# Moving the output weights ahead of group 3, loading two groups ahead of the DMA transposes, and 64-token blocks from group 3 on, in a fused linear-attention and SwiGLU kernel

## The chip, the cores and the metric

One core of a Trainium2 chip runs the whole program. The metric is the device time of one execution in microseconds (us). Most executions of a kernel agree within a per cent or so; some fall into a slower state. Each run is therefore marked fast or slow, and ratios use fast runs alone. A quoted median is of all runs; where some were slow, the text says so.

## The reference, cut to what matters

Batch 4, 8 heads, 768 tokens, head size 64. A linear attention with a decay per head works through the tokens in blocks of 64. Its output, 3072 tokens of 512 columns, goes through a SwiGLU feed-forward (FFN) of width 1536.

```python
for b in range(nb):                       # blocks of 64 tokens
    intra = einsum('bhic,bhjc->bhij', qb, kb) * Dmask
    intra = einsum('bhij,bhjd->bhid', intra, vb)
    inter = einsum('bhid,bhde->bhie', qb * lam_pow, kv_state)
    out[:, :, sl] = intra + inter
    kv_state = lam_block * kv_state + einsum('bhsd,bhse->bhde', kb * rev_pow, vb)
...
g = x @ w_gate; val = x @ w_val
return (g * sigmoid(g) * val) @ w_out
```

## The kernel before

A *group* is 256 tokens of one batch; there are 12. The FFN works on tiles of two groups (512 tokens), six tiles in all. TensorE runs the FFN of one tile while the attention of later groups is put in between as short insertions. To prepare a group, k, q and v are loaded, k and q are cast (q also scaled), a DMA transpose turns them (the first three groups are turned on TensorE), and GpSimd scales v. Then TensorE computes scores and the state update ("ahead"), and later the part from the state ("inter") and the part inside the block ("intra"), together the "core".

Groups below `NAT0` use blocks of 128 tokens, made of two neighbouring tokens in each partition. Their loads are one DMA each with 512-byte pieces. Groups from `NAT0` on use blocks of 64 tokens. Their loads are ten DMAs a group (four for k, four for q, two for v) with 256-byte pieces:

```python
NAT0 = 6
def load_fp32(g, eng, src, what, h0=0, h1=H):
    ...
    if g < NAT0:                      # 128-token form: one DMA
        eng.dma_start(out=t[:, h0:h1], in_=gsrc(src, g, h0)[:, 0:h1 - h0])
        return
    ...
    parts = [(0, 128, False)] if what == "v" else [(0, M, False), (M, M, True)]
    for s in range(2):                # 64-token form: 2 or 4 DMAs
        for p0, n, rev in parts:
            eng.dma_start(out=t[p0:p0 + n, :, s * D:s * D + D], in_=...)

def dma_transpose(g):                 # in the sync queue, with all loads
    nc.sync.dma_start(out=tt..., in_=t..., transpose=True)

def cast_scaled(g, eng=nc.vector):
    nc.scalar.copy(out=..., in_=st[("kraw", g)]...)          # k, on ACT
    eng.tensor_tensor(out=..., in0=st[("qraw", g)]..., ...)  # q, on VectorE
    dma_transpose(g)

def ffn_out(t, b, last=False):        # output projection and store
    ... 12 matmuls of 512 columns ...
    fn(out=osb[:, c0:c1], in_=ps)     # ACT
    eng.dma_start(out=..., in_=osb)   # ACT's queue, 256 KB

# the plan: at(step, what to do after it)
at(s0[5], load_group, 3)
at(s0[7], load_group, 4, "kq")
at(s0["11b"], cast_scaled, 3, nc.gpsimd)
at(s1a[3], cast_scaled, 4)
at(s1a[3], load_group, 5)
for c in range(0, FC, 2):
    at(s1a[3], wo_piece, c, c + 2)    # output weights behind load 5
...
at(s1b[6], ahead, 4)
at(s1b[8], wo_cast, ACTC)             # the cast that ACT waits for
at(s1b[10], core_b, 4)
```

## Time and profile before

| | before |
|---|---|
| median | 229.23 us (228.62 to 229.84) |
| span of the profiled run | 227.1 us |
| TensorE busy | 96% |
| mean granted TensorE clock | 1.000 |
| idle of TensorE at attention pieces, in all | 1.7 us on ACT's guard copy, 1.2 of it once |

The prediction below shows most lines of this profile as it reads them. On the page, the clock that the throttle granted to TensorE, one digit for each of 40 slices, is full all the way:

```profile
PEclk9999999999999999999999999999999999999999
```

### The profile page before, as it was taken

To read this page: it belongs to the slowest core of one execution; us is meant where nothing else is said; L and a number is where in the kernel's file an instruction comes from. 1 tells how busy PE (TensorE), PEld (TensorE's weight loads), DVE (VectorE), ACT (ScalarE), POOL (GpSimd) and SP (SyncE) were. 2 spreads that over 40 slices of the span, in tenths; PEclk is the share of its full clock that TensorE was granted. 3 is DMA by queue.
4 is the path that set the end of the run, shared out by engine and by line. 5 is a ranking of instruction groups with operands and counts; after the bars stand their busy time and mean duration, and the time that the engine had idled before them with its cause. 6 is when DMAs were issued, how large, how long until landed. Compare 5 with 4: busy or idle time off the path is not lost.

```text
span 227.1 us, 5890 instructions
## 1 busy us (share of the span) xinstructions
PE 218.5 (96%) x2432; PEld 118.2 (52%) x2444; DVE 90.1 (40%) x154; ACT 106.5 (47%) x209; POOL 88.2 (39%) x129
## 2 busy tenths in 40 slices
PE   7889999999979999999999999999999999999994
PEld 3556455878854444454544544544544444444443
DVE  2754357685825214545352362253242123222200
ACT  5868585754652446363454463453433423322221
POOL 6476736642793312978373092092150000000000
PEclk9999999999999999999999999999999999999999
DMA  6999999899997779799877748815101101101122
GB/s 199 345 360 377 367 354 313 210 255 352 300 219 189 206 168 222 177 200 191 217 178 186 185 98 214 214 36 139 49 3 48 46 3 46 46 0 46 49 92 92
DMA packets 88012, 39.70 MB, mean 175 GB/s; under 512 B 57650, under 2 KB 83506, under 8 KB 87986
## 3 DMA queue, kind: packets, MB, share of 16 engines
q1 hardware_dynamic: 83474, 32.64, 55.2%
q10 hardware_dynamic: 4512, 6.69, 8.3%
q8 instruction: 19, 0.31, 0.5%
q14 instruction: 7, 0.06, 0.1%
HBM read 28.31 MB, written 6.29 MB: 152 GB/s over the span
## 4 chain that ended last, share of the span: by engine, by line
PE 84%; DMA 6%; SPq 5%; issue 1%; DVE 1%; ACT 1%; DVEq 0%; ACTq 0%
PE bank L539 27%; PE bank L517 25%; PE bank L524 24%; DMA woraw<-in_moe_w_out_dram 4%; DMA qraw<-in_q_dram 2%; PE bank L475 2%; SPq L99 2%; SPq L228 2%; PE bank L462 2%; PE bank L383 1%; PE bank L353 1%; PE bank L327 1%; PE bank L290 1%; DVE ssb L334 1%; PE bank L168 0%
## 5 line engine op out<-in xcount | busy, mean ns | idle before, releaser
L527 DVE TENSOR_TENSOR h<-sil,bank 128x512 bf16<-128x512 bf16 (+1 forms) x87 | 51.4, 595 | 110.7 <-PE bank L524 94.5
L517 PE MATMUL bank<-xt,wg_sb 128*128 128x512 bf16 (+1 forms) x348 | 76.7, 343 | 0.0
L524 PE MATMUL bank<-xt,wv_sb 128*128 128x512 bf16 (+1 forms) x348 | 76.5, 342 | 0.0
L521 ACT ACTIVATE sil<-bank 128x512 bf16<-128x512 f32 (+1 forms) x87 | 45.8, 528 | 43.4 <-PE bank L517 40.4
L539 PE MATMUL bank<-wo_sb,h 128*128 128x512 bf16 (+1 forms) x288 | 64.2, 370 | 0.7 <-issue 0.2
L524 PEld LDWEIGHTS <-wv_sb 128*128 128x128 bf16 x348 | 34.0, 98 | 28.3
L517 PEld LDWEIGHTS <-wg_sb 128*128 128x128 bf16 x348 | 32.2, 98 | 27.4 <-DVE xt L487 0.5
L539 PEld LDWEIGHTS <-h 128*128 128x128 bf16 x300 | 29.1, 98 | 32.4
L541 ACT COPY osb<-bank 128x512 f32<-128x512 f32 (+1 forms) x24 | 13.8, 576 | 54.9 <-PE bank L539 52.9
L239 POOL TENSOR_TENSOR v_s<-v,dec 128x1024 bf16<-128x1024 f32 (+1 forms) x14 | 23.2, 1665 | 13.9 <-DMA v<-in_v_dram 9.5
L422 POOL TENSOR_TENSOR kvf<-kvs,ups 128x256 f32<-128x256 f32 x8 | 5.8, 726 | 45.1 <-ACT ups L405 40.1
L334 DVE TENSOR_TENSOR ssb<-bank,causal 128x512 bf16<-128x512 f32 x24 | 15.5, 684 | 3.9 <-PE bank L327 3.8
L487 ACT CAST xt<-bank 128x512 bf16<-128x512 f32 x21 | 12.8, 665 | 3.1 <-PE bank L475 2.3
L422 POOL TENSOR_TENSOR kvf<-kvf,ups 128x256 f32<-128x256 f32 x16 | 13.4, 839 | 0.6
L431 POOL CAST kvn<-kvf 64x256 bf16<-64x256 f32 x24 | 11.6, 483 | 1.5
L405 ACT COPY ups<-bank 128x256 f32<-128x256 f32 (+1 forms) x24 | 9.5, 450 | 2.3 <-PE bank L383 1.4
L259 ACT CAST qk<-kraw 128x1024 bf16<-128x1024 f32 x9 | 9.4, 1043 | 0.0
L261 DVE TENSOR_TENSOR qk<-qraw,qdn 128x1024 bf16<-128x1024 f32 x6 | 7.7, 1286 | 3.7 <-DMA qraw<-in_q_dram 3.7
L475 PE MATMUL bank<-ssb,v_s 64*64 64x128 bf16 (+1 forms) x384 | 7.2, 208 | 2.0 <-ACT guard L446 1.7
L222 POOL CAST wv_sb<-wraw 128x1024 bf16<-128x1024 f32 (+1 forms) x7 | 6.4, 918 | 6.1 <-DMA wraw<-in_moe_w_val_dram 6.0
L358 DVE TENSOR_TENSOR ssb<-bank,causaln 128x512 bf16<-128x512 f32 x12 | 8.3, 688 | 1.2 <-PE bank L353 1.1
L233 POOL CAST wo_sb<-woraw 128x1024 bf16<-128x1024 f32 x5 | 5.7, 1171 | 5.3 <-DMA woraw<-in_moe_w_out_dram 5.3
(62 smaller groups left out, 115.6 us busy)
## 6 DMA issues: line engine op xcount, KB each, us to landing
out_dram<-osb ACTq DMA_DIRECT2D x23, 256.0 KB, 2.5
v<-in_v_dram SPq DMA_DIRECT2D x16, 256.0 KB, 4.2
woraw<-in_moe_w_out_dram SPq DMA_DIRECT2D x6, 512.0 KB, 7.1
kraw<-in_k_dram SPq DMA_DIRECT2D x24, 128.0 KB, 3.2
qraw<-in_q_dram SPq DMA_DIRECT2D x24, 128.0 KB, 3.8
wraw<-in_moe_w_gate_dram SPq DMA_DIRECT2D x5, 512.0 KB, 6.6
wraw<-in_moe_w_val_dram SPq DMA_DIRECT2D x5, 512.0 KB, 7.3
kraw<-in_k_dram SPq DMA_DIRECT2D x4, 512.0 KB, 6.5
```

Of the source, the lines that this page charges most:

```text
L239: eng.tensor_tensor(out=st[("vs", g)][:, h0:h1], in0=st[("v", g)][:, h0:h1].rearrange("p h (s d) -> p h s d", s=2), in1=vfac(g, h0, h1), o ...
L334: nc.vector.tensor_tensor(out=ssb[:, h2, 2 * c:2 * c + 2].rearrange("p a s n -> p a (s n)"), in0=sp[(c, h2)].rearrange("p (a x) -> p a x", ...
L422: nc.gpsimd.tensor_tensor(out=o, in0=f, in1=u, op=ALU.add)
L431: nc.gpsimd.tensor_copy(out=o[64 - h2 * 64:128 - h2 * 64], in_=f[h2 * 64:h2 * 64 + 64])
L475: nc.tensor.matmul(op[r][h2 * 64:h2 * 64 + 64, cols(g, hp, s)], v_s[ps, 2 * hp + h2, s], ssb[ps, h2, hp * 2 + s] if g >= NAT0 else ssb[ps, ...
L487: fns[r](out=xt[:, g % 2, :, r].rearrange("p h (m s) -> p h s m", s=2) if g < NAT0 else xt[:, g % 2, :, :, r * M:r * M + M], in_=op[r].rea ...
L517: nc.tensor.matmul(gp[:, 0:N], wg_sb[:, mc, fs], xt[:, b0 // 2:b1 // 2, mc].rearrange("p g b n -> p g (b n)"), start=(mc == 0), stop=(mc = ...
L521: nc.scalar.activation(sil[:, 0:N], gp[:, 0:N], AF.Silu)
L524: nc.tensor.matmul(vp[:, 0:N], wv_sb[:, mc, fs], xt[:, b0 // 2:b1 // 2, mc].rearrange("p g b n -> p g (b n)"), start=(mc == 0), stop=(mc = ...
L527: nc.vector.tensor_tensor(out=h_sb[:, fc, b0:b1].rearrange("p b n -> p (b n)"), in0=sil[:, 0:N], in1=vp[:, 0:N], op=ALU.mult)
L539: nc.tensor.matmul(ps, h_sb[:, fc, b], wo_sb[:, fc, c0:c1], start=(fc == 0), stop=(fc == FC - 1))
L541: fn(out=osb[:, c0:c1], in_=ps)
```

## The change

The intent is to take away ACT's wait for the output weights (they come before the loads of group 3), to keep loads two whole groups ahead, and to use the cheaper 64-token insertions for groups 3 to 5 as well. The diff, cut to its core (lines that only release delayed copies, and the value scaling of group 4, are left out as well):

```diff
-    NAT0 = 6
+    NAT0 = 3
@@ cast_scaled
         dma_transpose(g)
+        load_group(g + 2)
@@ plan
-    at(s0[5], load_group, 3)
+    for c in range(0, FC, 2):
+        at(s0[5], wo_piece, c, c + 2)
-    at(s0[7], load_group, 4, "kq")
+    at(s0[7], load_group, 3)
+    at(s0[7], load_group, 4)
...
-    at(s0["11b"], cast_scaled, 3, nc.gpsimd)
-    at(s1a[3], cast_scaled, 4)
-    at(s1a[3], load_group, 5)
-    ... (scores, core and state of groups 3 to 5 in pieces)
+    at(s1a[8], cast_scaled, 3)
+    at(s1a[8], v_scale, 3, nc.gpsimd)
+    at(s1a[8], ffn_out, 0, 0)
+    at(s1a[8], ffn_out, 0, 1)
+    at(s1a[8], ffn_out, 0, 2)
+    at(s1a[8], ahead, 3)
+    at(s1a[8], cast_scaled, 4)
+    at(s1a[8], ffn_out, 0, 3)
+    at(s1a[10], core, 3, SPLIT)
+    at(s1b[5], ahead, 4)
+    at(s1b[2], cast_scaled, 5)
+    at(s1b[6], v_scale, 5, nc.gpsimd)
+    at(s1b[11], cast_scaled, 6)
+    at(s1b[11], ffn_out, 1, 0)
+    at(s1b[11], attend, 4)
+    at(s1b[11], v_scale, 6, nc.gpsimd)
+    at(s1b[11], ffn_out, 1, 1)
+    ... (the other projections, attend 5; the casts of wo spread over step 1a)
```

In the queue that gives: output weights, load 3, load 4, transpose 3, load 5, transpose 4, load 6 and so on. Group 3 is the first of its batch and has no state yet, so the change also skips the state matmuls that would multiply by zero.

More of the change, by code (lines that the diff above doesn't have):

```diff
@@ L244, in load_group @@
     def load_group(g, parts="kqv"):
+        if g >= NG:
+            return
         for src, what in ((k, "kraw"), (q, "qraw"), (v, "v")):
@@ L394, in upd_copy @@
         hd = "p (h d) -> p h d"
-        if i == 0 and 0 in parts:
+        if i == 0 and g >= NAT0:
+            st[("kv", g)] = [None]
+        elif i == 0 and 0 in parts:
             kv = kv_pool.tile([128, HP, D], BF16, name="kvn", tag="kvn1", bufs=2)
@@ L455, in inter @@
         started = set()
-        for hp, s, r, h2 in phase(g, first, (1,) if i == 0 else (0, 1) if first else (1, 0)):
+        for hp, s, r, h2 in phase(g, first, (1,) if i == 0 and g < NAT0 else (0, 1) if first else (1, 0)):
             if g < NAT0 and s:
@@ L459, in inter @@
             n = 2 * s + r if g >= NAT0 else r
+            if kv[n] is None:
+                continue
             row, hq = (1 - h2, HP - 1 - hp) if g >= NAT0 and r else (h2, hp)
@@ L477, in intra @@
                              ssb[ps, h2, hp * 2 + s] if g >= NAT0 else ssb[ps, h2, hp, s],
-                             start=((first or (i == 0 and r == 0)) and (r, h2) not in started),
+                             start=((first or (i == 0 and r == 0 and g < NAT0)) and (r, h2) not in started),
                              stop=(not first), skip_group_check=True)
@@ L556, in attend @@
             upd_copy(g + 1)
-            scores(g + 1)
+            if g + 1 >= NAT0:
+                scores(g + 1)
             late, later[:] = later[:], []
         core_b(g)
-        if g + 1 < NG:
+        if g + 1 < NAT0:
+            scores(g + 1)
+            state(g + 1)
+        elif g + 1 < NG:
             later[:] = late
@@ L684, in _body @@
     at(s0["11a"], core, 2, SPLIT)
-    at(s0["11b"], cast_scaled, 3, nc.gpsimd)
-    at(s0["11b"], v_scale, 3, nc.gpsimd)
     at(s0["11b"], state, 2)
-    at(s0["11b"], load_group, 4, "v")
+    at(s0["11b"], wo_cast)
     s1a = [step(1, fc, 0, 2) for fc in range(FC)]
     s1b = [step(1, fc, 2, 4) for fc in range(FC)]
-    at(s1a[3], cast_scaled, 4)
-    at(s1a[3], load_group, 5)
-    for c in range(0, FC, 2):
-        at(s1a[3], wo_piece, c, c + 2)
-    at(s1a[7], scores, 3, (0,))
-    at(s1a[7], run_later, 2)
@@ L698, in _body @@
-    at(s1a[8], scores, 3, (1,))
-    at(s1a[8], upd_mm, 3)
-    at(s1a[8], run_later, 2)
-    at(s1a[8], upd_copy, 3)
-    at(s1a[9], core_a, 3)
-    at(s1a[10], core_b, 3, SPLIT)
-    at(s1a[10], v_scale, 4, nc.gpsimd)
-    at(s1a[10], state, 3)
-    at(s1b[3], cast_scaled, 5)
-    at(s1b[3], load_group, 6)
-    at(s1b[4], wo_cast)
-    at(s1b[4], wo_cast)
-    at(s1b[6], ahead, 4)
-    at(s1b[6], run_later, 2)
-    at(s1b[6], wo_cast)
-    at(s1b[6], wo_cast)
-    at(s1b[6], v_scale, 5, nc.gpsimd)
@@ L715, in _body @@
-    at(s1b[8], wo_cast, ACTC)
-    at(s1b[8], wo_cast)
-    at(s1b[9], core_a, 4)
-    at(s1b[10], core_b, 4)
-    at(s1b[11], ffn_out, 0, 0)
-    at(s1b[11], ahead, 5)
-    at(s1b[11], run_later, 3)
-    at(s1b[11], ffn_out, 0, 1)
-    at(s1b[11], core_a, 5)
-    at(s1b[11], ffn_out, 0, 2)
-    at(s1b[11], core_b, 5)
+    at(s1a[1], wo_cast)
+    at(s1a[3], wo_cast, ACTC)
+    at(s1a[4], wo_cast)
+    at(s1a[5], wo_cast, ACTC)
+    at(s1a[6], wo_cast)
+    at(s1a[8], cast_scaled, 3)
+    at(s1a[8], v_scale, 3, nc.gpsimd)
@@ L726, in _body @@
+    at(s1a[8], ffn_out, 0, 0)
+    at(s1a[8], ffn_out, 0, 1)
+    at(s1a[8], ffn_out, 0, 2)
+    at(s1a[8], ahead, 3)
+    at(s1a[8], run_later, 2)
+    at(s1a[8], cast_scaled, 4)
+    at(s1a[8], ffn_out, 0, 3)
+    at(s1a[10], core, 3, SPLIT)
+    at(s1a[11], v_scale, 4, nc.gpsimd)
+    at(s1b[5], ahead, 4)
+    at(s1b[2], cast_scaled, 5)
+    at(s1b[6], v_scale, 5, nc.gpsimd)
     at(s1b[11], cast_scaled, 6)
-    at(s1b[11], load_group, 7)
+    at(s1b[11], ffn_out, 1, 0)
+    at(s1b[11], attend, 4)
@@ L728, in _body @@
+    at(s1b[11], run_later, 2)
     at(s1b[11], v_scale, 6, nc.gpsimd)
-    at(s1b[11], ffn_out, 0, 3)
-    outs = [(1, b) for b in range(4)]
+    at(s1b[11], ffn_out, 1, 1)
+    at(s1b[11], ffn_out, 1, 2)
+    at(s1b[11], ffn_out, 1, 3)
+    at(s1b[11], attend, 5)
+    outs = []
     for t in range(2, NG // 2):
-        sn = [step(t, fc) for fc in range(FC)]
         if t == 2:
-            at(sn[2], ahead, 6)
-        for j, g in ((3 if t == 2 else 0, 2 * t + 3), (7 if t == 2 else 6, 2 * t + 4)):
+            sn = [step(t, fc, 0, 2) for fc in range(2)] + [step(t, fc, 2, 4) for fc in range(2)]
+            sn = sn[2:] + [step(t, fc) for fc in range(2, FC)]
+        else:
+            sn = [step(t, fc) for fc in range(FC)]
+        for j, g in ((0, 2 * t + 3), (6, 2 * t + 4)):
@@ L737, in _body @@
             if g < NG:
                 at(sn[j], cast_scaled, g)
-                if g + 1 < NG:
-                    at(sn[j], load_group, g + 1)
                 at(sn[1 + j], v_scale, g, nc.gpsimd)
         if t + 1 < NG // 2:
-            at(sn[6 if t == 2 else 4], attend, 2 * t + 2)
+            at(sn[4], attend, 2 * t + 2)
             at(sn[10], attend, 2 * t + 3)
```

## The prediction

> **What bounds the kernel now.** I read the page first, then the chain that ended last, then one engine at a time: the TensorE timeline for what each attention piece costs, the sync queue for loads and transposes, GpSimd for the state sums. From the page:
>
> ```profile
> PE 218.5 (96%) x2432; PEld 118.2 (52%) x2444; DVE 90.1 (40%) x154; ACT 106.5 (47%) x209; POOL 88.2 (39%) x129
> PE 84%; DMA 6%; SPq 5%; issue 1%; DVE 1%; ACT 1%; DVEq 0%; ACTq 0%
> ```
>
> TensorE is the bound, and not by its busy share alone: in the chain 84% is TensorE. Dense matmuls follow each other at 0.86 us for four of 512 columns, so 0.216 us each. The FFN needs 6 tiles x 144 of them, 864 x 0.216 = 186.6 us. Of the 227.1 us span, about 16 us lie before the first and 3 us after the last; the rest, some 22 us, is attention pieces between dense matmuls, plus waits. The only wait of note in that stretch is in the chain of waits and in ACT's timeline:
>
> ```profile
> 54.98 9.45 DMA woraw<-in_moe_w_out_dram
> 64.67 0.74 issue
> 65.88 0.64 PE bank L475 x32
> ```
>
> ```profile
> 64.45 1.04 ACT L233 CAST wo_sb<-woraw 128x1024 bf16<-128x1024 f32 x1 [2.24 <-DMA woraw<-in_moe_w_out_dram]
> 65.68 0.15 ACT L446 COPY guard<-bank 128x1 f32<-128x1 f32 x1
> ```
>
> ACT sat for an output-weight load; behind it stood the guard copy that the attention matmuls of group 4 wait for. TensorE lost 1.21 us there (the idle before that piece in its timeline).
>
> Next, two neighbouring insertions on TensorE, group 5 in the 128-token form, group 6 in the 64-token form:
>
> ```profile
> 70.02 0.45 PE L383 MATMUL bank<-v_s,qk 64*64 64x64 bf16 x32
> 70.30 0.62 PE L327 MATMUL bank<-qkt 64*64 64x128 bf16 x32
> ```
>
> ```profile
> 87.84 0.45 PE L383 MATMUL bank<-v_s,qk 64*64 64x64 bf16 x32
> 88.12 0.46 PE L353 MATMUL bank<-qkt 64*64 64x64 bf16 x32
> ```
>
> Measured as the distance between the dense matmuls on either side, less what the dense ones need, the first pair costs 0.92 us and the second 0.76.
>
> The sync queue, in order, shows what a 64-form group costs to load, and the windows view how fast:
>
> ```profile
> 80.16 1.81 SPq L252 DMA_TRANSPOSE qkt<-qk  x1
> 82.50 2.74 SPq L106 DMA_DIRECT2D kraw<-in_k_dram  x4
> 85.34 3.14 SPq L106 DMA_DIRECT2D qraw<-in_q_dram  x4
> 88.53 1.53 SPq L106 DMA_DIRECT2D v<-in_v_dram  x2
> ```
>
> ```profile
> 28.00:34.00 6.00, 6.00 (x42) 3.19 (x40) 2.86 (x7) 4.98 (x9) 2.59 (x4) 1.00 1.10 353
> 98.00:100.00 2.00, 2.00 (x131) 1.61 (x131) 1.29 (x2) 1.15 (x4) 0.69 (x2) 1.00 1.30 243
> ```
>
> The last column is GB/s: 353 with packets of 512 and 1024 bytes, 243 with the 256-byte packets of a 64-form group, both with the DMA engines full. Last, GpSimd for the state of a 64-form group and the value scaling queued behind it:
>
> ```profile
> 90.78 0.72 POOL L422 TENSOR_TENSOR kvf<-kvf,ups 128x256 f32<-128x256 f32 x1
> 91.56 0.40 POOL L433 CAST kvn<-kvf 128x256 bf16<-128x256 f32 x1
> 91.92 1.70 POOL L422 TENSOR_TENSOR kvf<-kvf,ups 128x256 f32<-128x256 f32 x1
> 96.44 1.91 POOL L239 TENSOR_TENSOR v_s<-v,dec 128x1024 bf16<-128x1024 f32 x1
> ```
>
> From the state matmuls at 87.84 to the end of this scaling at 98.35 it is 10.5 us; without the slow addition 9.5.
>
> **What the Trainium skill says.** "DMA: Bandwidth & Descriptors", section "Why small descriptors are slow (HBM only)": a 256-byte descriptor pays a fixed overhead per packet. The trace agrees: 18 ns for a 256-byte packet, 27 for one of 512, and 243 against 353 GB/s. The same page, "Queues, rings and completion order": on each engine descriptors are consumed in ring order. It agrees: the transpose issued at 58.73, behind the output weights, held the queue for 6.84 us. "SBUF — State Buffer", section "SBUF: two separate sides": GpSimd and a VectorE operation with two SBUF inputs share a port pair as an exclusive lock. It agrees: the addition of 1.70 us instead of 0.72 began within 0.2 us of VectorE's scaling of q, 1.31 us at 91.73. "TensorE: Matmul & The Clock Gate", section "HAM oscillation": TensorE idle for over about 3.4 us falls back to half clock. This trace has no such gap after the start and grants the full clock; it matters only if a new wait is that long.
>
> **The change part by part.** *Blocks of 64 for groups 3 to 5.* Insertion costs before, from the TensorE timeline: group 3 in four pieces 0.44 + 0.73 + 0.44 + 0.67 = 2.28; group 4 0.92 + 0.70 + 0.73 = 2.35 (the wait taken off); group 5 0.92 + 0.66 + 0.89 = 2.47; scores and state of group 6 0.76. Sum 7.9. After: state and scores of 3, 0.76; the core of 3, some 1.2 (the last group's, inter and intra alone, takes 1.19); state and scores of 4, 0.76; two merged insertions for groups 4 and 5, of which the second has the scores of 6, at 1.5 (groups 6 and 7: 1.55 and 1.41). Sum 5.7. Gain 2.2 us.
>
> *Output weights ahead of group 3.* The wait goes: 1.2 us. Together 3.4, so 225.8 us if nothing new waits. Splitting two steps of tile 2 into halves costs nothing (0.44 against 0.86 us for four matmuls), and the output projections are only moved.
>
> *The loads.* This is where I expect the gain to go. Through the values of group 2 the queue is unchanged; they land at about 34.5. Then 3.1 MB of output weights at 353 GB/s, 8.9 us: 43.4. Then groups 3 and 4, both ahead of the transpose of 3 in the same queue, 3.1 MB in 256-byte packets at 243: 12.9 us, so 56.3; two output stores of 256 KB go through the same engines, about 1 us: 57.3. The transpose lands some 2.6 us after what is in front (108.08 issued, 110.05 landed, the loads before it at 107.5): 59.9. TensorE wants it sooner: the step after which it needs it ends at 48.3 (its half step 7 ends at 47.4 now, plus 0.87), three output projections of 12 x 0.216 take 7.8, the state matmuls 0.35: 56.4. **Wait of 3.5 us at the scores of group 3**, by my estimate between 1.5 and 5.
>
> For the later groups, transpose plus load hold the queue 1.8 + 7.8 = 9.6 us, so the following transposes land near 69, 79, 88 and 98; the scores of 4 to 7 would be wanted at 69, 78, 87 and 97.5 without that wait, and 3.5 later with it. So the first wait pays for the others.
>
> *GpSimd.* The scaling of the values of group 5 stands behind the state of 4: 9.5 to 10.5 us after the state matmuls of 4. TensorE has 0.76 + 6 half steps 5.2 + one projection 2.6 + 0.3 = 8.9 us of other work. For group 6: 1.2 + 7.8 + 0.3 = 9.3; for group 7: 1.2 + 8.7 + 0.3 = 10.2. Waits of about 0.6 to 1.6, 0 to 1.2 and 0 to 0.3; I take 1.3 us in all, since not every chain meets VectorE on the port.
>
> Sum: 229.2 - 3.4 + 3.5 + 1.3 = 230.6.
>
> **Rivals.** (a) *No new wait, the gain stays*: 225.8. For it: the three projections were put between cast and scores, which looks like cover made to measure, and my load times rest on one saturated rate. Against: the bytes add up to 57 us whichever way they are ordered in front of that transpose. (b) *The waits I name*: 230.6. (c) *The wait grows and cools TensorE*: if group 3 comes 5 us late, the half clock for about 3.4 us adds 1.7 by the page's figure, and GpSimd's upper values add 1.8 more: 229.2 - 3.4 + 5 + 1.7 + 3.1 = 235.6. For it: 256-byte loads ran at 222 GB/s elsewhere (the window from 114 to 118 us), which alone is 1.2 us. (d) *Hidden anyway*: the 1.2 us wait could be replaced by another one on ACT, as the cast of group 3 now stands in front of the projections' copies; with eight banks TensorE can run three projections ahead, so I give it little.
>
> **Range and chances.** I lean a little towards (a), since the arrangement looks tuned: 230.2, with a range from 225.8 (all of the gain) to 233.8. Faster by 2% would be under 224.6, more than the whole gain: 0.03. Slower by 2% is over 233.8, which wants most of (c): 0.12. Within 2%: 0.85.
>
> **What would show it.** Right: in the TensorE timeline the scores of group 3 (lines of 64-column matmuls) preceded by 2 to 5 us idle near 56 us, ended by the transpose; the transpose issued after the v load of group 4, at 53 us or later; the state matmuls of groups 5 and 6 preceded by under 2 us each, ended by GpSimd's scaling; no idle at the intra matmuls of group 4 on ACT's guard; the merged insertions near 1.5 us. Wrong: loads of groups 3 and 4 at well over 243 GB/s or landed before 53 us, no idle at those scores (then the time is near 226), or TensorE's granted clock under full after 56 us (then it is above 233).

## More of the kernel before

In the sync queue's own waits (total us, times, longest), loads waited for output stores, though TensorE did not feel it:

```profile
SPq L106 <- DMA out_dram<-osb: 4.9, 3, 3.0
```

## The result and the profile after

The changed kernel takes **245.71 us** (median of 4 fast runs, 242.93 to 246.36); the kernel before took 229.19 beside it. The ratio is 1.070, with a 95% interval from 1.061 to 1.078. Ratios here are the mean time of one kernel's fast runs over that of the other's of the same rounds, so not quite the ratio of the medians quoted. The prediction was 230.2 with a range to 233.8: it was wrong.

The page of the changed kernel, first the engine's busy share, then the granted clock, then the shares of the chain that ended last:

```profile
PE 223.0 (91%) x2497; PEld 122.3 (50%) x2508; DVE 88.1 (36%) x151; ACT 108.4 (44%) x211; POOL 95.4 (39%) x146
...
PEclk9999999999579999958999999999999999999999
...
PE 76%; DMA 13%; POOL 6%; ACT 1%; issue 1%; DVE 1%; SPq 0%; POOLq 0%; DVEq 0%; ACTq 0%
```

TensorE's share of the chain fell from 84% to 76%, DMA rose from 6% to 13% and GpSimd entered with 6%. Twice the clock dips to about half, in the slices near 64 and 106 us. The TensorE timeline (start, duration, what, and in brackets the idle time before it with what ended it) has the two places, and one of the waits for GpSimd:

```profile
56.92 0.45 PE L386 MATMUL bank<-v_s,qk 64*64 64x64 bf16 x32
64.39 0.64 PE L356 MATMUL bank<-qkt 64*64 64x64 bf16 x32 [7.03 <-DMA qkt<-qk]
...
65.80 4.47 PE L546 MATMUL bank<-wo_sb,h 128*128 128x512 bf16 x10 [0.22 <-issue]
...
90.02 0.45 PE L386 MATMUL bank<-v_s,qk 64*64 64x64 bf16 x32 [1.55 <-POOL v_s L239]
...
105.20 0.64 PE L356 MATMUL bank<-qkt 64*64 64x64 bf16 x32 [5.16 <-DMA qkt<-qk]
...
107.03 1.06 PE L531 MATMUL bank<-xt,wv_sb 128*128 128x256 bf16 x4
```

L356 is the scores of a 64-token group. Those of group 3 wait 7.03 us and those of group 6 wait 5.16 us, each for its DMA transpose. After each wait TensorE is slow: ten projection matmuls take 4.47 us, where ten that followed each other took 2.32 just before. Four matmuls of 256 columns take some 0.85 us (starts at 106.21, 107.03 and 107.89) in place of 0.44.

Adding up these places gives the account of the loss. Waits: 7.03 + 5.16 + 1.55 + 0.28 + 0.75 = 14.8 us (the last three for GpSimd's value scaling, at groups 5, 6 and 2). Half clock: 11 projection matmuls at 0.21 us more each, the one at 64.97 with 0.4 more, and six sets of four 256-column matmuls after 106 us at 0.42 more each: 5.2 us. Less the gain of 3.4 that the prediction had, if it came in full: 16.6. The span grew by 244.6 - 227.1 = 17.5 us in the profiled runs. So nearly all of it is at these places.

Why the transposes were late is in the sync queue's timeline (start, time that the queue was held, what):

```profile
47.13 1.25 SPq L106 DMA_DIRECT2D v<-in_v_dram  x2
48.47 3.35 SPq L106 DMA_DIRECT2D kraw<-in_k_dram  x4
51.92 3.31 SPq L106 DMA_DIRECT2D qraw<-in_q_dram  x4
55.46 1.41 SPq L106 DMA_DIRECT2D v<-in_v_dram  x2
57.06 4.49 SPq L254 DMA_TRANSPOSE qkt<-qk  x1
...
90.75 3.13 SPq L106 DMA_DIRECT2D qraw<-in_q_dram  x4
93.98 1.19 SPq L106 DMA_DIRECT2D v<-in_v_dram  x2
95.34 4.82 SPq L254 DMA_TRANSPOSE qkt<-qk  x1
```

The transpose of group 3 is issued at 57.06 behind load 4, when TensorE already stands at its scores; it landed at 64.35. The output weights landed at 45.3 and the last of loads 3 and 4 at 61.0: 3.15 MB in 15.7 us, 200 GB/s. Two output stores of 256 KB landed in the same stretch. The transposes of groups 4, 5, 6 and 7 landed at 75.0, 86.6, 105.2 and 117.1.

The transpose of group 6 stands behind load 7, and in the middle of that load the queue had stood still, from 87.14 to 90.75. The sync queue's waits now have:

```profile
SPq L106 <- DMA out_dram<-osb: 12.3, 6, 3.6
```

The trace's DMA records name the completion semaphore of each transfer. In this program all DMAs of the sync queue and of ACT's queue take theirs from one set of eight, in turn. A load is issued only when the last user of its semaphore has landed, and that can be an output store on the other queue. (In 114 successive pairs whose first landing is in the trace, none was issued earlier.) Three such pairs, taken from the records:

```
store issued  landed   next load on the same semaphore issued
   70.92       74.66      74.68   (k of group 6)
   88.75       (none)     90.75   (q of group 7)
   97.01      104.19     104.21   (k of group 8)
```

So there is a loop: TensorE comes late to a projection, its store is late, the load that has the same semaphore is held, and so is the transpose behind it. The first and third pair show it to 0.02 us. In the second the landing is missing from the trace, so that one is inferred.

What remained of the prediction's gain is there too: ACT's wait for output weights is gone, and waits on ACT's guard copy sum to 0.8 us.

### The profile page after: what moved, and what is told of

Its sections match the earlier page's. It is cut to its first block, busy times and chain, and to the rows that moved or that the text cites. A ratio compares the mean times of both kernels' runs of the same rounds, so it can differ in the third digit from the quotient of the medians.

```text
span 244.6 us, 6085 instructions
## 1 busy us (share of the span) xinstructions
PE 223.0 (91%) x2497; PEld 122.3 (50%) x2508; DVE 88.1 (36%) x151; ACT 108.4 (44%) x211; POOL 95.4 (39%) x146
## 4 chain that ended last, share of the span: by engine, by line
PE 76%; DMA 13%; POOL 6%; ACT 1%; issue 1%; DVE 1%; SPq 0%; POOLq 0%; DVEq 0%; ACTq 0%
PE bank L546 24%; PE bank L524 22%; PE bank L531 21%; DMA qkt<-qk 7%; DMA wraw<-in_moe_w_val_dram 3%; DMA v<-in_v_dram 3%; PE bank L482 2%; POOL v_s L239 2%; POOL kvf L427 1%; PE bank L386 1%; PE bank L469 1%; PE bank L356 1%; PE bank L168 1%; PE bank L293 1%; POOL kvs L430 1%
## 5 line engine op out<-in xcount | busy, mean ns | idle before, releaser
L546 PE MATMUL bank<-wo_sb,h 128*128 128x512 bf16 (+1 forms) x289 | 66.3, 380 | 0.7 <-issue 0.2
L524 PEld LDWEIGHTS <-wg_sb 128*128 128x128 bf16 x356 | 34.2, 100 | 27.4 <-issue 0.5
L548 ACT COPY osb<-bank 128x512 f32<-128x512 f32 (+1 forms) x24 | 13.9, 577 | 62.8 <-PE bank L546 62.8
L361 DVE TENSOR_TENSOR ssb<-bank,causaln 128x512 bf16<-128x512 f32 x18 | 12.2, 687 | 32.7 <-PE bank L356 32.6
L436 POOL CAST kvn<-kvf 64x256 bf16<-64x256 f32 x34 | 16.6, 487 | 2.1
L427 POOL TENSOR_TENSOR kvf<-kvf,ups 128x256 f32<-128x256 f32 x22 | 16.8, 764 | 1.1
L356 PE MATMUL bank<-qkt 64*64 64x64 bf16 x288 | 4.9, 206 | 12.2 <-DMA qkt<-qk 12.2
L410 ACT COPY ups<-bank 128x512 f32<-128x512 f32 (+1 forms) x24 | 10.8, 503 | 3.0 <-PE bank L386 2.1
L263 DVE TENSOR_TENSOR qk<-qraw,qdn 128x1024 bf16<-128x1024 f32 x9 | 11.1, 1230 | 0.3 <-DMA qraw<-in_q_dram 0.3
L356 PEld LDWEIGHTS <-qkt 64*64 64x64 bf16 x288 | 3.9, 114 | 12.4 <-DMA qkt<-qk 12.4
L337 DVE TENSOR_TENSOR ssb<-bank,causal 128x512 bf16<-128x512 f32 x12 | 7.9, 682 | 1.6 <-PE bank L330 1.6
```

What stands on the lines that cost most here:

```text
L356: nc.tensor.matmul(sp[h2][rm, (hp * 2 + s) * M:(hp * 2 + s) * M + M], tt[dp, 0, s, hq, rm], tt[dp, 1, s, hq, rm], start=True, stop=True, s ...
L361: nc.vector.tensor_tensor(out=ssb[:, h2], in0=sp[h2].rearrange("p (a x) -> p a x", x=M), in1=bap(causaln, [[0, 2 * HP], [1, M]]), op=ALU.mult)
L427: nc.gpsimd.tensor_tensor(out=o, in0=f, in1=u, op=ALU.add)
L436: nc.gpsimd.tensor_copy(out=o[64 - h2 * 64:128 - h2 * 64], in_=f[h2 * 64:h2 * 64 + 64])
L524: nc.tensor.matmul(gp[:, 0:N], wg_sb[:, mc, fs], xt[:, b0 // 2:b1 // 2, mc].rearrange("p g b n -> p g (b n)"), start=(mc == 0), stop=(mc = ...
L546: nc.tensor.matmul(ps, h_sb[:, fc, b], wo_sb[:, fc, c0:c1], start=(fc == 0), stop=(fc == FC - 1))
```

## The experiments

The theory after reading the result was: the loss comes from two late transposes. The first is late because of the 64-token loads of groups 3 and 4 in front of it, the second because of the stores in the loads' ring of semaphores. The rivals were the half clock as a cause of its own, GpSimd, and the transposes being slow whatever stands before them. The two kernels are called "before" and "changed" below. The median of the kernel before lay between 228.8 and 229.7 us. The changed kernel was run in the first call only, so a difference in us between it and an experiment is one between calls.

### 1. Loads one group ahead

```diff
-        load_group(g + 2)        # in cast_scaled
+        load_group(g + 1)
-    at(s0[7], load_group, 4)
```

> Changed kernel, but the loads of group 4 are no longer put ahead of the transpose of group 3: each transpose is followed by the load of one group, not two ahead. Theory A (the transpose of 3 came late because the loads of 4, 9.8 us of queue and engine time, stood in front of it in the sync queue, and the rest follows from that wait): the transpose of 3 is issued near 53 us instead of 57.1 and lands before 58; the wait of 7.0 us at the scores of 3 shrinks under 1 us, the half-clock stretch after it (1.7 us) goes, and the second wait of 5.2 us at the scores of 6 shrinks too, since the queue is no longer held by stores that TensorE made late: 229 to 234 us. Theory B (the queue has too much to carry whatever its order: 256-byte loads at 200 GB/s plus transposes): the wait moves from group 3 to groups 4 to 6, with the same total: 242 us or more.

Measured: 236.11 us, ratio 1.029 (1.023 to 1.036). The transpose of group 3 was issued at 49.96 and TensorE did not wait for it. There was no half clock at that place. The time lies between the two expectations, as other waits came in TensorE's list (total, times, longest):

```profile
PE bank L356 <- DVE h L534: 3.2, 1, 3.2
PE bank L524 <- DVE xt L494: 1.7, 1, 1.7
```

In VectorE's timeline two casts of q came after 4.7 and 4.8 us of idle time. The first is ended by its load, which was issued from 55.05 on and landed at 62.56; the second is put down to GpSimd, so its cause is less sure. Behind each came the copies and products that TensorE then waited for. After the wait of 1.7 us, too, TensorE ran at half clock for a while (0.83 to 0.86 us for four matmuls of 256 columns, from 65.36 on). So load 4 in front of the transpose causes the first wait, but taking it away from there is no cure: two groups ahead had a use.

### 2. Dummy matmuls in the two waits

```diff
+        warm_into(sp[0], {3: 26, 6: 17}.get(g, 0), 512)   # in scores_n
```

> Changed kernel with dummy matmuls in the two long waits: 26 of 512 columns (5.6 us) just before the scores of group 3, 17 (3.7 us) before those of group 6, into the bank that the scores then overwrite. They change nothing that TensorE waits for. If the half clock after the two waits is caused by TensorE's idleness, the granted clock is full throughout and the stretches after the waits (11 matmuls of the projection in 4.5 us instead of 2.6; six half-steps at 0.86 instead of 0.44 us per four) run at full speed: 4 us less, about 241.5 us, with both transposes landing at about the same time. If the clock fell for another reason, the time stays at 245 to 246.

Measured: 243.84 us, ratio 1.063 (1.057 to 1.069). The result stays correct, as the dummies' bank is overwritten. The first dip of the clock is gone and the second is smaller:

```profile
PEclk9999999999999999979999999999999999999999
```

The second still costs some 1.7 us (five sets of four matmuls from 104.80 to 108.65), so the dummies took away some 3.6 of the 5.2 us of half clock. By the medians 1.9 us came back; the two intervals overlap (1.057 to 1.069 here, 1.061 to 1.078 for the changed kernel), so even that is not clear of noise. From dense matmul to dense matmul the first insertion took 8.26 us (8.14 in the changed kernel), the second 8.30 (7.42). The transposes are what ends these stretches, and a TensorE at full clock only reaches the second one earlier and waits longer there. So the half clock is real, but by the medians about half of what was taken away went into the next wait; it does not carry the loss by itself.

### 3. The changed schedule with groups 3 to 5 in 128-token form

```diff
-    NAT0 = 3
+    NAT0 = 6
```

> Changed kernel with groups 3 to 5 kept in the 128-token form; the schedule alone is changed. Their loads are then 3 transfers of 512-byte packets for a group instead of 10 of 256-byte ones. If the slow loads of the 64-token form are what makes the transpose of 3 late: 3.1 MB for groups 3 and 4 in about 9 us instead of 15.7, the transpose lands near 58, the wait at the scores of 3 is under 1.5 us, the waits for the value scaling of group 5 (1.55 us) goes as its state has 2 additions instead of 4; about 231 us (before's time, less its 1.2 us wait, plus 2 to 3 of new waits). If the order of the queue alone is to blame, the wait at the scores of 3 stays over 4 us and the time over 238.

Measured: 233.14 us, ratio 1.018 (1.012 to 1.023). This one line brings back 12.6 of the 16.5 us. Loads 3 and 4 now end 9.3 us after the output weights (42.23 to 51.52, so 339 GB/s). In the sync queue, load 4 and the transpose of group 3:

```profile
42.34 1.40 SPq L99 DMA_DIRECT2D kraw<-in_k_dram  x1
43.83 1.69 SPq L99 DMA_DIRECT2D qraw<-in_q_dram  x1
45.57 1.39 SPq L99 DMA_DIRECT2D v<-in_v_dram  x1
50.23 2.35 SPq L254 DMA_TRANSPOSE qkt<-qk  x1
```

The transpose is issued when its cast is done, 6.8 us earlier, and the first wait is gone. The scores of group 6, a 64-token group in both, still wait 2.46 us, and half clock follows there (four matmuls of 512 columns take 1.69 us in place of 0.86). The line takes the whole form away and not its loads alone: the waits for GpSimd's scaling of groups 5 and 6 go with it, and so does the gain of 2.2 us by shorter insertions that the prediction counted.

### 4. GpSimd's value scaling ahead of the state

```diff
+    at(s1b[4], v_scale, 5, nc.gpsimd)
     at(s1b[5], ahead, 4)
-    at(s1b[6], v_scale, 5, nc.gpsimd)
+    at(s1b[11], v_scale, 6, nc.gpsimd)
     at(s1b[11], ffn_out, 1, 0)
     at(s1b[11], attend, 4)
-    at(s1b[11], v_scale, 6, nc.gpsimd)
```

> Changed kernel with the value scalings of groups 5 and 6 issued on GpSimd before the state sums of 4 and 5, not behind them. The waits of TensorE for them (1.55 us before the state matmuls of group 5, 0.28 of group 6) go. If the wait for the transpose of group 6 hides behind them it grows by as much and the time stays within 0.5 us of 245.7; if it does not, the time falls by up to 1.8 us to 244.

Measured: 244.54 us, ratio 1.066 (1.059 to 1.073). The waits on the value scaling fell from 2.6 us to 0.2, and those on transposes grew from 12.2 to 13.8. So GpSimd's waits were real, as predicted, but sat ahead of the longer wait: taking them away moved the time little.

### 5. 64-token blocks from group 3 on, on the schedule of before

```diff
-    NAT0 = 6
+    NAT0 = 3
     ... (scores of 3 in one piece, no state matmuls for it, its state before its core)
```

> The kernel before with nothing changed but the form: groups 3 to 5 in blocks of 64 tokens (both halves of the scores of 3 in one insertion, and its state sum moved ahead of its core, as that form needs). My count of TensorE's time gives a gain of 0.7 us for each of the three groups, 2.1 in all, if the loads hide: 227 us. If the slow 256-byte loads and the ten transfers for a group are themselves too much for this stretch (which is what the run with the new schedule and the old form suggests, 233.1 against 245.7), there are new waits for group 3 or the output weights behind the longer loads of 3 to 5 (some 4 us more queue time for each): 233 us or more.

Measured: 244.01 us, ratio 1.065 (1.057 to 1.072). The 64-token blocks alone, without any reordering of loads, cost as much as the whole change. Here, however, the waits are mostly on GpSimd's state sums, at the inter matmuls of groups 3 to 5:

```profile
PE bank L466 <- POOL kvn L433: 5.5, 12, 0.9
PE bank L466 <- POOL kvn L435: 3.2, 3, 1.1
```

The granted clock was 0.972 in this run, so half clock is part of its loss too. A 64-token group needs three intermediate states and not one, and the schedule of before gives GpSimd little time between the state matmuls and the core. The changed plan removes this wait. So this run does not show the cause of the changed kernel's loss, but it shows that the 64-token form has a second price, which that plan had been made to hide.

### 6. The first output tiles stored from GpSimd's queue

```diff
-            eng.dma_start(out=bass.AP(tensor=out.tensor, ...
+            (nc.gpsimd if t < 2 else eng).dma_start(out=bass.AP(tensor=out.tensor, ...
```

> Changed kernel with the output stores of tiles 0 and 1 issued from GpSimd, not ACT. In the compiled program loads and stores share a ring of eight completion semaphores in turn, so that a load can be made to wait for the landing of a store that TensorE has not got to; the sync queue's waits name stores with 12.3 us in 6 waits. If that holds the transpose of group 6 back: those waits go (under 5 us), the transpose of 6 is issued 3 us or more earlier than 95.3, the second wait of TensorE shrinks from 5.2 to under 3 us, and the time falls by 3 to 5 us to 241 to 243 (less of it if GpSimd, which has its own chain of states, is slowed by the issuing). If the queue is merely full, the second wait stays within 1 us of 5.2 and the time at 244 to 247.

Measured: 238.73 us (one of four runs slow, the others 236.44 to 239.14), ratio 1.039 (1.031 to 1.047). In the trace these stores have eight semaphores of their own. The sync queue's waits for stores fell from 12.3 us in six to:

```profile
SPq L106 <- DMA out_dram<-osb: 4.2, 2, 3.0
```

The transpose of group 6 in the sync queue, and all of TensorE's waits for transposes:

```profile
87.85 4.96 SPq L254 DMA_TRANSPOSE qkt<-qk  x1
...
PE bank L356 <- DMA qkt<-qk: 5.5, 1, 5.5
```

The transpose of group 6 was issued at 87.85 and not at 95.34, and its wait of 5.16 us is gone; the wait at group 3 was 5.5. So the second long wait, with its half clock, comes from stores that hold loads. By the medians the edit is worth 7.0 us; 1.5 of it, in the two profiles, is the shorter wait at group 3.

### 7. Only ACT's wait taken away, on the kernel before

```diff
-    at(s1b[8], wo_cast, ACTC)
-    at(s1b[8], wo_cast)
     at(s1b[9], core_a, 4)
     at(s1b[10], core_b, 4)
+    at(s1b[10], wo_cast, ACTC)
+    at(s1b[10], wo_cast)
```

> The kernel before with one edit: the last two casts of output weights (one on ACT, one on GpSimd) stand behind the core of group 4 instead of two steps ahead of it. If ACT's wait for that load is what held the guard copy and so TensorE, its 1.2 us go and nothing takes their place: 228.0 us, ratio 0.995. If the weights are then late for the first projection, TensorE waits there instead and the time stays at 229.

Measured: 227.70 us (227.43 to 230.1, 6 runs) against 228.9; ratio 0.996 (0.991 to 1.002). The guard wait is down to 0.5 us in all, and a new one of 0.7 us appears at the first projection, for the cast now made later. It is the lowest median, but the interval includes 1, so it is not shown to beat the kernel before.

### 8 and 9. Output weights ahead of load 5, alone, and with 64-token blocks from group 5 on

```diff
-    at(s1a[3], load_group, 5)
     for c in range(0, FC, 2):
         at(s1a[3], wo_piece, c, c + 2)
+    at(s1a[3], load_group, 5)
     ... (casts of wo at steps 2 to 7 of 1b; cast and load of the next groups after them)
```

The second of the two adds `NAT0 = 5` and moves the core of group 5 behind two more projections.

> The kernel before, all groups in their old form, with the output weights alone moved ahead in the queue: in front of the load of group 5 instead of behind it, the cast of group 5 five half-steps later, two projections exchanged with pieces of group 5. It tests that one part of the change by itself. The load of 5 in the old form is 3 transfers, 1.5 MB at 350 GB/s, so its transpose should be in time: 1.2 us less than before, 228.0. If the transpose of 5 or 6 is late, as it was by 1.6 us in the run with group 5 in the new form, 229 to 230.

> An attempt to keep what is worth keeping: the schedule of before with the output weights ahead of the load of group 5 only, group 5 alone of the three in 64-token blocks, its cast later, and two projections of tile 1 moved ahead to cover its state. Gain 1.2 us of the ACT wait, 0.7 of the form: 227.3 us if no transpose is late; if the transpose of 5 or 6 is late (its load starts some 3 us later and takes 4 us longer), 229 to 232.

Measured: 228.49 us, ratio 1.000 (0.996 to 1.003), and 229.58 us (two of six runs slow), ratio 0.999 (0.992 to 1.006). Moving the output weights forward costs nothing and gains nothing that can be measured: ACT's long wait goes, but waits on the guard copy still sum to 1.2 us. One more 64-token group is neutral as well when it is group 5 alone, though its profile has 2.0 us of waits for transposes, 1.6 of them at one place.

### 10. Only k of load 4 in front of the transpose

```diff
-    at(s0[7], load_group, 4)
+    at(s0[7], load_group, 4, "k")
         dma_transpose(g)
+        if g == 3:
+            load_group(4, "qv")
         load_group(g + 2)
```

> Changed kernel with only a part of the load of group 4 moved behind the transpose of group 3: its q and its values (6 of 10 transfers, two thirds of the bytes), k stays in front. If what stands in front of that transpose sets its time, it is issued some 5 us sooner than 57.1 (near 52), the wait of 7.0 us at the scores of 3 falls to about 2, the half clock after it (1.7 us) goes: 239 us, less what the later load of 4 costs in turn through the in-order cast of its q on VectorE (1 to 2 us). If the transpose is held by something else, the wait stays over 5 us and the time over 243.

Measured: 240.43 us, ratio 1.050 (1.044 to 1.056). The transpose of group 3 was issued at 50.20 and its wait fell to 0.9 us. The waits came back at the groups behind it:

```profile
PE bank L358 <- DMA qkt<-qk: 10.5, 5, 3.7
```

The profile before this edit had 12.2 us in two such waits; now it is 10.5 in five. Moving the bytes behind the first transpose only moves them in front of the next. This is against the prediction's view that the first wait pays for the others: even with little of a first wait, the later transposes are late.

### 11. Experiments 4 and 6 together, without and with dummies

The edits are those shown above; the second run adds 22 dummies at group 3.

> Changed kernel with the stores of tiles 0 and 1 from GpSimd (238.7 us alone) and the value scalings of 5 and 6 ahead of the states (244.5 alone, where the wait for the transpose of 6 grew by what the scaling gave back). With that second wait gone, the scalings should now count in full: 1.6 + 0.3 us less than 238.7, so 236.8. If the wait for the transpose of 6 comes back by as much, 238 or more.

> The same with 22 dummy matmuls (4.7 us) in the wait at the scores of 3, to keep TensorE warm there. In the run with both waits filled the clock stayed full but only 1.9 us came back, since the next transpose then came as late as before; with no second wait behind it the half clock after the first should count: 1.5 us or so less than the run without dummies, 235.3. If the time does not fall, the half clock was hidden behind something after it all the same.

Measured: 236.60 us, ratio 1.035 (1.030 to 1.040). GpSimd's waits are gone, and waits on transposes are 8.8 us in three, 6.2 of them at group 3. With the dummies: two of four runs were slow; the fast ones took 239.15 and 235.69 (ratio 1.038, 1.030 to 1.047). That second run, whose profile is of a slow run, is inconclusive; it gives no sign of a gain.

### 12. The transposes from ACT's queue, alone and with experiments 4 and 6

```diff
-        nc.sync.dma_start(out=tt..., in_=t..., transpose=True)
+        nc.scalar.dma_start(out=tt..., in_=t..., transpose=True)
```

> The changed kernel, with one edit: the eight DMA transposes are issued from ACT's queue and not from the sync queue. The loads of the next group but one still stand in the same places in the program, but a transpose need no longer wait behind them in its own queue. Theory 'queue order' (the transposes come late because they stand behind two groups of loads, and behind stores through these): the transpose of group 3 is issued near 50 us, when the cast is done, and lands well before 57; the first wait of 7.0 us falls under 1.5, the second under 3, no half clock: 229 to 235 us. Rival 'capacity' (the 16 engines are full with 256-byte packets and a transpose gets through only when the loads are done, from whatever queue): the transpose is issued near 50 but lands after 60, the first wait stays at 4 us or more: 240 us or more.

> As the run before it (transposes from ACT's queue), and also the first output tiles stored from GpSimd's queue and the value scalings of groups 5 and 6 put ahead of the state additions. If all three waits of the changed kernel (transpose of 3, transpose of 6, value scaling) are separate causes, and each edit takes its own, the time is the prediction's version without new waits, 225.8 to 228.5, and would beat the kernel before. If the loads themselves are the limit from group 4 on, 230 to 236 with a wait on a transpose of 2 us or more left.

Measured: 246.33 us (two of four runs slow, the others 242.82 and 246.01), ratio 1.069 (1.060 to 1.077), and 239.77 us, ratio 1.048 (1.043 to 1.053). The profile of the first is of a slow run; only its order of events is used. ACT's timeline and TensorE's have:

```profile
50.99 3.75 ACTq L254 DMA_TRANSPOSE qkt<-qk  x1
```

```profile
59.87 0.45 PE L356 MATMUL bank<-qkt 64*64 64x64 bf16 x32 [2.47 <-DMA qkt<-qk]
```

The transpose is issued at 50.99, 6 us earlier than in the changed kernel, yet TensorE gets it only at 59.87; the wait falls from 7.03 to 2.47. The fast profile of the second run agrees: issued at 50.43, scores at 59.01 after a wait of 2.18. So both theories were half right. Some 4.6 us of the first wait is order in the queue. The rest is likely the engines, which work on transpose and loads at once: in this second trace the transpose's 2048 packets of 256 bytes spread from 52 to 57 us, the loads' packets thinned out meanwhile, and its completion came only between 58.0 and 58.6. And there is a new cost that no theory had: the issue holds ACT's own instructions for 2.6 to 3.8 us, and TensorE then waits for ACT (3.70 us on a guard copy, 4.27 on a SiLU in the first run). Neither version beats the kernel before.

### 13. 128-token loads cut into ten transfers

```diff
+        if 3 <= g < NAT0:                    # on experiment 3 (NAT0 = 6)
+            n = 4 if what == "v" else 2
+            for h in range(0, H, n):
+                eng.dma_start(out=t[:, h:h + n], in_=gsrc(src, g, h)[:, 0:n])
+            return
```

> The earlier run with groups 3 to 5 again in 128-token form (233.1 us, loads of three transfers to a group, first wait gone), with these three groups' loads cut into ten transfers a group (four for k, four for q, two for v) of the same 512-byte packets and the same layout. It tells the number of transfers from the packet size as the reason why a 64-token group takes so long. Theory 'each transfer costs some 0.64 us of the queue whatever it moves': a group takes 6.4 us of the queue again, the transpose of 3 is issued after 54 us and the wait of 3 us or more at its scores returns: 236 to 242 us. Rival 'small packets': the wait stays under 1 us and the time within 1.5 us of 233.1.

Measured: 236.23 us, ratio 1.032 (1.027 to 1.037). One of the four runs was slow; the fast ones took 235.32 to 236.76, at the edge between the two expectations. Load 4 and the transpose of group 3 in the sync queue:

```profile
44.77 1.90 SPq L101 DMA_DIRECT2D kraw<-in_k_dram  x4
46.77 1.95 SPq L101 DMA_DIRECT2D qraw<-in_q_dram  x4
48.76 1.02 SPq L101 DMA_DIRECT2D v<-in_v_dram  x2
51.12 3.31 SPq L259 DMA_TRANSPOSE qkt<-qk  x1
```

A group takes about 5 us of the queue and not the 6.4 that a fixed price per transfer would have asked for; the wait at group 3 was 1.05 us. From the landing of the output weights to that of load 4 it was 12.0 us (42.58 to 54.61, 261 GB/s). With 9.3 us for three transfers a group of the same pieces, and 15.7 for ten of half the size, the 6.4 us that the 64-token form costs here split into **2.7 for the number of transfers and 3.7 for the rest**, for which the packet size is the likely reason. But the two stores in the stretch of 15.7 us are in that rest (none landed in the 9.3 us), and the placing of k and q in the partitions differs as well; these were not told apart. The split is also rough: it rests on one profile each, and in four other runs with the same queue the stretch of 15.7 us took 14.9 to 16.5.

### 14. Both cures at once

Experiment 3 (`NAT0 = 6`) with experiment 6 (stores of the first two tiles from GpSimd's queue).

> The changed kernel with both edits that removed a transpose wait each: groups 3 to 5 in 128-token form (alone 233.1 us; its wait at the scores of 6, 2.5 us, is still there) and the stores of the first two output tiles issued from GpSimd's queue (alone 238.7 us; it took the wait at the scores of 6 away and left that of group 3). If the two transpose waits have separate causes, the edits add: the wait at the scores of 6 falls under 0.5 us, no half clock, and the time is 228 to 230.5, the kernel before within 1%; that is, the rest of the change (order of output weights, casts and projections) is worth nothing either way. If the second wait is a follow-on of the queue's length and not of the stores, it stays over 1.5 us and the time over 231.5.

Measured, with five rounds: 230.79 us, ratio 1.000 (0.994 to 1.007). That median is of six runs, two of them slow; the four fast ones lie between 228.65 and 231.66. The profile, of a slow run, has 2.4 us of waits for transposes left, 2.0 of them now at group 5 and 0.4 at group 6:

```profile
PE bank L356 <- DMA qkt<-qk: 2.4, 2, 2.0
```

With both causes out, the whole loss is gone, while the rest of the change (output weights first, casts moved up, loads two ahead, projections moved) is still in. So these two causes, with what follows from them, account for the loss. What inside the 64-token form makes the first of them is less sure: experiment 13 shows the number of transfers to cost some 3 us of time by the medians, and the remaining 9.5 or so of the 12.6 us were not divided further. Alone the two edits were worth 12.6 and 7.0 us by the medians, together the whole 16.5: they overlap by some 3 us, probably since a TensorE that is late at group 3 also stores late.

## Why the prediction was wrong

**What held.** ACT's wait is gone. Net of waits and half clock the new insertions cost close to what was worked out: the core of group 3 measured 1.22 us (1.2 predicted), state and scores of group 4 0.76 (0.76), and the merged one of group 4 3.08 - 1.55 = 1.53 (1.5). That the whole gain of 3.4 us arrives in the time is not shown: taking away ACT's wait alone gave no measurable gain (experiments 7 and 8). The first wait was named at the right instruction, with the right releaser, and with the check "the transpose issued after the v load of group 4, at 53 us or later". GpSimd's waits were also named; they summed to 2.6 us and not 1.3. Of these 0.75 was at group 2, whose values landed at 35.63 in this profile. With the same queue up to there they landed at 34.57 in experiment 2, and this wait was not there; so it belongs to the run and not to the change.

**The first step that failed, by its size:** "groups 3 and 4 ... 3.1 MB in 256-byte packets at 243: 12.9 us". It took 15.7 us, where the prediction had 13.9 with the stores. The rate came from a window in which the DMA engines were full. In front of this transpose they were not: between 44 and 46 us they were busy for 0.29 of the time and between 46 and 50 for 0.84 to 0.89, as the queue issued its twenty transfers one by one (most k and q transfers of 128 KB held it for 0.63 to 0.64 us); between 50 and 61, where they were full, 247 GB/s came, stores included. The output weights also landed 1.9 us later than "43.4" (in five other runs with the same queue up to there at 43.0 to 44.7, so part of this is the run), and the transpose landed 3.4 us after the loads in front of it and not 2.6. That 2.6 came from one transpose, which the prediction misread as issued at 108.08, the end of its hold of the queue (it was issued at 105.38); the transpose before it had landed 5.5 us after its loads (93.2 and 98.67). TensorE came at 57.35 (56.4 predicted). So the wait was 3.5 + 1.9 + 1.8 + 0.8 - 0.95, about 7.03 us, beyond the stated 1.5 to 5.

**The step that failed in kind:** "transpose plus load hold the queue 1.8 + 7.8 = 9.6 us ... So the first wait pays for the others." The transposes came 10.7, 11.5, 18.6 and 11.9 us after each other. A transpose behind loads held the queue for 3.1 to 4.8 us and not 1.8, and loads stood up to 3.6 us at a time for output stores. The prediction took the cycle from a stretch in which stores did not disturb, and counted them as bytes ("about 1 us") but not as something the queue waits for. The waits of 4.9 us for stores were in the profile of before; they cost TensorE nothing there, as the loads were early enough. Experiments 6 and 14 show that they are the second cause. Experiment 10 shows that making the first wait short does not make the others go.

**The term that was in a rival only:** the half clock. Rival (c) had it, with one wait of 5 us and 1.7 us of loss. Two waits of over 5 us gave 5.2 us of loss, and the prediction's own sign of being wrong, "TensorE's granted clock under full after 56 us (then it is above 233)", is what came. In experiment 2, taking some 3.6 us of it away brought back 1.9 by the medians, which is not clear of noise. Nor did the half clock matter only where a wait is over 3.4 us, as the prediction took it: it followed waits of 1.7 us (experiment 1) and 2.46 us (experiment 3) too.

**The range.** The prediction gave slower by 2% a chance of 0.12, since that "wants most of (c)". But the parts of (c) were not independent: a late TensorE makes late stores, late loads, late transposes and then a later TensorE.

**What stays open.** Whether the transposes' own time beside loads (2.2 us of wait even from their own queue) could be shortened was not tried. Nor was a 64-token form with fewer transfers. No version was shown to beat the kernel before.

## What to carry to other kernels

Before moving loads in front of something that they share a queue with, count transfers as well as bytes, and take the rate from a stretch with the same sort of transfers issued one by one, not from one where the engines are full. Then list what those loads themselves wait for, even where that wait costs nothing today: slack in one queue hides a dependence on another engine's stores, which becomes a loop once the slack is spent. When a long wait also cools TensorE, fill it once to see what the cold is worth by itself; here it was some 1.9 us of 16.5, not clear of noise.

## What the Trainium skill lacked or had wrong

- No page has it: in a program like this one DMAs of two queues can share a small set of completion semaphores in turn, so that loads on one queue wait for stores on the other. Here the loads waited 12.3 us in six waits, one load going out 0.02 us after a store had landed, and with the stores on a third queue the time fell from 245.7 to 238.7 us.
- "DMA: Bandwidth & Descriptors", section "Why small descriptors are slow (HBM only)", explains the loss by overhead per packet and per descriptor; it does not say what part the number of transfers has. Here that mattered as well: 3.15 MB took 9.3 us as three transfers a group, 12.0 as ten with the same 512-byte pieces, and 15.7 (two stores included) as ten with 256-byte pieces.
- "DMA: Bandwidth & Descriptors", section "DMA Transpose (X-bar)", gives no time for one transpose among loads. Here one of 512 KB held its queue for 1.6 us where it stood free of loads (at 113.28) and for 3.1 to 4.8 behind them, landed up to 9.8 us after its issue (95.34 to 105.16), and held ACT's instructions for 2.6 to 3.8 us when issued there.
